# Issuing the decay tables' transfers from ScalarE, ahead of further loads, in a linear-attention and MLP kernel

## Chip, cores and metric

The kernel runs on one core of a Trainium2 chip. The metric is the device time of one execution in microseconds (us). Three runs of the kernel before took 560.29, 560.22 and 559.4 us; the median is 560.22 us.

## What is computed

Three stages stand one behind the other. The first is causal linear attention with decay, for 2 batches of 8 heads, 768 positions and 64 values per head:

```
intra = (q_b k_b^T * Dmask) v_b            # Dmask[i, j] = lam ** (i - j), zero above the diagonal
inter = (q_b * lam ** (i + 1)) kv_state
kv_state = lam ** block * kv_state + (k_b * lam ** (block - 1 - j))^T v_b
```

Each head has its own `lam`, between 0.97 and 0.99. The 1536 x 512 result goes through a gated layer, `(x w_a * x w_b) w_out` with 1536 hidden columns, and through a second layer, `max(x w1, x w2, x w3) w_out` with 768. All is float32; the weights reach the kernel as raw 64-bit words.

## The kernel before, in words

Attention works in 12 chunks (`order`): 2 batches of 6 chunks of 128 positions, all 8 heads at once. A chunk needs four tiles of 256 KB: queries and keys with the head dimension on the partitions (`q`, `k`), keys with positions on the partitions (`n`) and values (`v`). For chunk n, `scores(n)` (L145) multiplies q and k on TensorE; `masked(n)` (L173) multiplies the scores by the decay mask `dmask` on VectorE, one half (even heads, odd heads) at a time, into two tiles `a`; `side(n)` (L156) makes the decayed queries `qs` (from `ltab`) and keys `kd` (from a column of `dmask`) on GpSimd; `values(n)` (L183) multiplies `a` by v (L190), adds the decayed queries times the running state `st` (L194), and makes the state's update `kv` from kd and v (L200). Behind it ScalarE copies the output tile (`xh`, L206), VectorE takes the remainder (`xl`, L207) and sums the state (`std`, L211 or L213), and ScalarE copies it to `st` (L215), which the next chunk's L194 reads. In TensorE's order the first three scores stand first, then values of chunk 0, scores of chunk 3, values of chunk 1, scores of chunk 4, and so on. VectorE's order is the masks of chunks 0, 1 and 2 (six instructions) before `xl` and `std` of chunk 0. Below, q0, k0 and so on are the loads of chunk 0, and "scores of chunk 4" is `scores(4)`.

From chunk 3 on VectorE, ScalarE and GpSimd also split weight tiles into two parts each (L72 to L81), and from chunk 5 on the first layer's products (`up1`, L92) are laid between the chunks. Behind attention only the layers' matmuls are left, with the splits beside them.

The decay tables start from `lam` (L310). `powers()` computes on VectorE a table `tab` of 8 x 256 values (L104 to L113) and stores it to DRAM as `tab_d` (L114, 8 KB). `tables()` (L119) reads it back in shifted windows, as two halves of `dmask`, each 128 partitions with 4 runs of 512 bytes (L122). `decay_rows()` (L124) reads rows broadcast over 64 partitions, twice, into `ltab` (L126).

Every transfer is issued by SyncE (SP in the profile) in the order of the program. The order is written out by hand (`manual_schedule`, from L309). At the head of the program it is: lam, q0, k0, q1, k1, q2, tab_d, k2, v0, the two mask halves, n0, q3, k3, the two `ltab` halves, v1, n1, v2, n2; then, from the loop, q4, k4, v3, n3, and so on.

Two kinds of wait stand ahead of an issue. One is for data: the store of `tab_d` waits for VectorE, and the first mask transfer waits until `tab_d` has landed. The other comes from the framework: it gives the transfers eight completion semaphores in turn, in the order of the program and counted over all issuing engines of this kind together (SyncE and ScalarE), and a transfer that takes up a semaphore waits until the transfer eight before it has landed. An engine that waits at one issue holds back all that it issues behind it.

Of the kernel before, what the change touches and what calls it, by code (L numbers as in the profile page):

```python
# [16 lines left out]
C = 128  # L17
NC = S // C
NP = H // 2
# [14 lines left out]
def decay_attention_gated_mlps(ctx: ExitStack, tc: tile.TileContext, qkv: bass.AP, lam: bass.AP, wts: bass.AP, out: bass.AP):  # L34
    nc = tc.nc
# [13 lines left out]
    def rd(t):  # L49
        return t.bitcast(F32)  # L50

# [1 line left out]
    raw, split = {}, {}  # L53
    state = {"raw": 0, "split": 0}

# [6 lines left out]
            state["raw"] += 1  # L62

    def split_to(u):
        """float64 to float32, bit by bit; what is below float32's normal numbers, told by the upper word read as a float32, becomes zero."""
        while state["split"] <= min(u, NUNIT - 1):
            n = state["split"]
            load_to(n)
            bits = raw.pop(n).bitcast(I32).rearrange("p (n two) -> p n two", two=2)
            low, high = bits[:, :, 0], bits[:, :, 1]  # L70
            w = wp.tile([128, 512], I32, tag="w", name=f"w{n}")
            nc.vector.tensor_scalar(out=w, in0=high, scalar1=3, scalar2=0x3FFFFFF8, op0=ALU.logical_shift_left, op1=ALU.bitwise_and)  # L72
            nc.vector.scalar_tensor_tensor(out=w, in0=low, scalar=29, in1=w, op0=ALU.logical_shift_right, op1=ALU.bitwise_or)  # L73
            nc.vector.scalar_tensor_tensor(out=w, in0=high, scalar=-0x40000000, in1=w, op0=ALU.bitwise_and, op1=ALU.bitwise_or)  # L74
            size = wp.tile([128, 512], F32, tag="s", bufs=2, name=f"ws{n}")
            nc.scalar.activation(out=size, in_=high.bitcast(F32), func=AF.Abs)  # L76
            t = w.bitcast(F32)
            nc.vector.scalar_tensor_tensor(out=t, in0=size, scalar=SMALLEST, in1=t, op0=ALU.is_ge, op1=ALU.mult)  # L78
            hi, lo = t2k(f"wh{n}", F32R), t2k(f"wl{n}", F32R)
            nc.scalar.activation(out=hi, in_=t, func=AF.Copy)  # L80
            nc.gpsimd.tensor_tensor(out=lo, in0=t, in1=rd(hi), op=ALU.subtract)  # L81
            split[n] = (hi, lo)
            state["split"] += 1

    def passes(out_ap, terms):
        """Sum of products of operands in two parts each, without the part below float32."""
        todo = []
        for (wh, _), (xh, xl) in terms:
            todo += [(wh, xh), (wh, xl)]
        todo += [(wl, xh) for (_, wl), (xh, _) in terms]  # L90
        for n, (w, x) in enumerate(todo):
            nc.tensor.matmul(out_ap, w, x, start=n == 0, stop=n == len(todo) - 1)  # L92

# [1 line left out]
    lam_sb = const.tile([H, 1], F32, name="lam_sb")  # L95
    tab = const.tile([H, 2 * C], F32, name="tab")
    pw = const.tile([H, 16], F32, name="pw")
# [2 lines left out]
    tab_d = dp.tile([H, 2 * C], F32, name="tab_d")  # L100

    def powers():
        """tab[h, C - 1 + n] = lam ** n; pw holds lam ** m - 1 for m = 1, 2, 4, ..."""
        nc.vector.memset(tab[:, 0:C - 1], 0.0)  # L104
        nc.vector.memset(tab[:, C - 1:C], 1.0)
        nc.vector.tensor_scalar(out=pw[:, 0:1], in0=lam_sb, scalar1=-1.0, scalar2=None, op0=ALU.add)
        o, m, n = C - 1, 1, 0
        while m < C:
            r = pw[:, n:n + 1]
            nc.vector.scalar_tensor_tensor(out=pw[:, n + 1:n + 2], in0=r, scalar=2.0, in1=r, op0=ALU.add, op1=ALU.mult)  # L110
            nc.vector.scalar_tensor_tensor(out=tab[:, o + m:o + 2 * m], in0=tab[:, o:o + m], scalar=r, in1=tab[:, o:o + m], op0=ALU.mult, op1=ALU.add)
            m, n = 2 * m, n + 1
        nc.vector.tensor_scalar(out=tab[:, o + m:o + m + 1], in0=pw[:, n:n + 1], scalar1=1.0, scalar2=None, op0=ALU.add)  # L113
        nc.sync.dma_start(out=tab_d, in_=tab)  # L114

    def view(offset, ap):
        a = tab_d[:, :]
        return bass.AP(tensor=a.tensor, offset=a.offset + offset, ap=ap)

    def tables():  # L120
        for g in range(2):
            nc.sync.dma_start(out=dmask[:, g], in_=view(g * 2 * C, [[1, 128], [4 * C, NP], [1, C]]))  # L122

    def decay_rows():  # L124
        for hh in range(2):
            nc.sync.dma_start(out=ltab[64 * hh:64 * hh + 64], in_=view(hh * 2 * C + C, [[0, 64], [4 * C, NP], [1, C]]))  # L126

# [1 line left out]
    x = [(xp.tile([128, KD, TT], F32R, tag="x", name=f"xh{t}"), xp.tile([128, KD, TT], F32R, tag="x", name=f"xl{t}")) for t in range(NTT)]  # L129
    st = const.tile([128, NP, 128], F32, name="st")  # L130
    std = const.tile([128, NP, 64], F32, name="std")
# [4 lines left out]
    def load(n, *which):  # L136
        if n >= len(order):
            return
        b, c = order[n]
        for i in which:  # L140
            t = t2k(f"{('q', 'k', 'n', 'v')[i]}{n}")
            nc.sync.dma_start(out=t, in_=qkv[b * NC + c, i])
            ld.setdefault(n, [None] * 4)[i] = t
# [10 lines left out]
        sc[n] = banks  # L154

    def side(n):  # L156
        """What a chunk needs besides its scores: queries and keys times powers of lam."""
        if n >= len(order):
            return
        b, c = order[n]  # L160
        q, k, kn, v = ld[n]
        kd = qs = None
        if c > 0:
            qs = t2k(f"qs{n}")
            nc.gpsimd.tensor_tensor(out=qs, in0=q, in1=ltab.rearrange("p a i -> p (a i)"), op=ALU.mult)
        if c < NC - 1:
            kd = t2k(f"kd{n}")
            nc.gpsimd.tensor_tensor(
                out=kd.rearrange("p (h d) -> p h d", h=H), in0=kn.rearrange("p (h d) -> p h d", h=H),
                in1=dmask[:, :, :, C - 1:C].rearrange("p g a i -> p (g a) i").to_broadcast([128, H, D]), op=ALU.mult)  # L170
        ld[n] = (qs, kd, v)
# [44 lines left out]
            if c < NC - 2:  # L216
                nc.vector.tensor_tensor(out=stt, in0=std, in1=ltab[:, :, C - 1:C].to_broadcast([128, NP, 64]), op=ALU.mult)

# [1 line left out]
    def split_psum(ps, hi, lo):  # L220
        nc.scalar.activation(out=hi, in_=ps, func=AF.Copy)
        nc.vector.tensor_tensor(out=lo, in0=ps, in1=rd(hi), op=ALU.subtract)
# [84 lines left out]
            nc.sync.dma_start(out=out[i * 128:i * 128 + 128, s], in_=ob[:, s])  # L307

    with tc.manual_schedule():  # L309
        nc.sync.dma_start(out=lam_sb, in_=lam)  # L310
        for n in range(2):
            load(n, 0, 1)
        load(2, 0)
        warm = t2k("warm", BF16)
        nc.vector.memset(warm, 0.0)
        nc.scalar.activation(out=warm[:, 0:1], in_=warm[:, 0:1], func=AF.Copy)
        ps = bank("warm_ps")
        for i in range(9):
            nc.tensor.matmul(ps, warm[:, 0:128], warm, start=True, stop=True)
        nc.gpsimd.memset(st, 0.0)  # L320
        powers()
        load(2, 1)
        load(0, 3)
        tables()
        load(0, 2)
        load(3, 0, 1)
        decay_rows()
        load(1, 3, 2)
        load(2, 3, 2)
        for n in range(3):  # L330
            scores(n)
        for n in range(2):
            masked(n)
            side(n)
        plan = [(f, t) for t in range(NTT) for f in range(4)] + [(f, t) for f in range(4, K1) for t in range(NTT)]
        for n in range(len(order)):
            load(n + 4, 0, 1)
            load(n + 3, 3, 2)
            load_to((-1, 0, 1, 2, 4, 6, 8, 9, 10, 11, 12, 13)[n])
            if n > 0:  # L340
                scores(n + 2)
            side(n + 2)
            masked(n + 2)
            values(n)
            for i in range(2):
                split_to((-1, -1, -1, 0, 1, 3, 5, 7, 9, 10, 11, 12)[n] - 1 + i)
                if n >= 5 and i == 0:
                    up1(*plan.pop(0))
        for f, t in plan:
            room = 2 * f + (58 - 3 * (f + 1)) // 2  # L350
            split_to(max(2 * f + 1, min(state["split"], room)))
            load_to(state["split"] + 1)
            if f == K1 - 1 and t > 0:
                split_g(0, 2 * t - 2)
                split_g(0, 2 * t - 1)
            up1(f, t)
            if t == NTT - 1:
                for v in (2 * f, 2 * f + 1):
                    split.pop(v)
        u = 2 * K1  # L360
        for t in range(NTT):
            down1(t, u, 2)
        for k in range(K1):
            split.pop(u + k)
        u += K1
        for f in range(K2):
            split_to(u + 3 * f + 2)
            for t in range(NTT):
                split_to(u + 3 * f + (3 + t if f < K2 - 2 else 3 + 2 * t if f < K2 - 1 else 6 + t))
                load_to(u + 3 * f + 6 + 2 * t)  # L370
                up2(f, t, u)
            for i in range(3):
                split.pop(u + 3 * f + i)
        u += 3 * K2
        for i in range(NT // 128):
            split_to(u + 5)
            down2(i, u)
# [47 lines left out]
```

## Time and profile before

| | us |
|---|---|
| median of three runs | 560.22 |
| lowest and highest run | 559.4, 560.29 |
| profiled execution, span from first to last instruction | 558.3 |
| TensorE busy in it | 541.5 |
| VectorE busy | 289.0 |
| ScalarE busy | 161.0 |
| GpSimd busy | 103.6 |

For the profiled execution only the span is recorded; the times of the runs also hold what lies around the span, 1.92 us at the median. A "busy" TensorE is not one at its peak, since its matmuls are pipelined. The times below are us from the start of the span. A transfer "lands" when its completion is seen; its issue is the short instruction on the queue of the engine that starts it (SPq for SyncE).

### The profile page before, as it was taken

The page shows a single profiled execution, that of the slowest core. Times are in us where ns is not written, and L with a number is a line of the kernel's source. Part 1 is how long each engine was busy: PE and PEld are TensorE (multiplying, and loading weights), DVE is VectorE, ACT ScalarE, POOL GpSimd, SP SyncE. Part 2 cuts the span into 40 slices and gives each one's busy share as a digit, 9 for nine tenths or more (in the row PEclk, how much of TensorE's full clock was granted, in tenths as well). Part 3 has the DMA queues.
Part 4 walks back from the last instruction along what each step waited for, and adds up shares of the span by engine and source line. Part 5 has one row for each costly group of instructions (what it writes and reads, how often), then busy time and mean ns, then how long its engine had stood idle before and what let it go on. Part 6 is the DMA issues. An engine that isn't in the chain of part 4 may idle for free.

```text
span 558.3 us, 7132 instructions
## 1 busy us (share of the span) xinstructions
PE 541.5 (97%) x2811; PEld 446.1 (80%) x2811; DVE 289.0 (52%) x452; ACT 161.0 (29%) x286; POOL 103.6 (19%) x85
## 2 busy tenths in 40 slices
PE   6998889999999999999999999999999999999997
PEld 3876677888888888888888888888888888888886
DVE  2788887676555542134748264124545556774000
ACT  1343334332323322123325152212232323332111
POOL 0735342222212220000110000000011112221000
PEclk9899999999999999999999999999999999999999
DMA  7986442232322321000211111001122112211112
GB/s 226 348 324 217 160 143 76 101 111 92 113 84 105 101 89 38 1 38 1 75 76 38 39 38 39 0 1 38 39 75 77 61 54 98 91 38 38 58 60 73
DMA packets 19089, 48.44 MB, mean 87 GB/s; under 512 B 2024, under 2 KB 3824, under 8 KB 19056
## 3 DMA queue, kind: packets, MB, share of 16 engines
q1 hardware_dynamic: 19056, 47.99, 24.8%
q8 instruction: 22, 0.36, 0.3%
q14 instruction: 11, 0.09, 0.0%
HBM read 44.83 MB, written 3.15 MB: 86 GB/s over the span
## 4 chain that ended last, share of the span: by engine, by line
PE 87%; DVE 5%; DMA 4%; issue 2%; ACT 1%; POOL 1%; SPq 1%; DVEq 0%; POOLq 0%; ACTq 0%
PE p L92 26%; PE y L269 18%; PE pa L92 16%; PE pb L92 16%; PE out L302 9%; DMA k<-qkv_dram 3%; DVE w L72 1%; PE o L194 1%; DVE w L73 1%; DVE w L74 1%; PE o L190 1%; DMA tab_d<-tab 1%; DVE w L78 1%; PE s L153 1%; POOL wl L81 0%
## 5 line engine op out<-in xcount | busy, mean ns | idle before, releaser
L81 POOL TENSOR_TENSOR wl<-w,wh 128x512 fp32r<-128x512 f32 x60 | 78.3, 1305 | 389.4 <-ACT wh L80 288.1
L80 ACT ACTIVATE wh<-w 128x512 fp32r<-128x512 f32 x60 | 37.9, 632 | 192.5 <-DVE w L78 185.5
L92 PE MATMUL p<-yh,wh 128*128 128x512 f32 x216 | 84.0, 389 | 0.0
L92 PE MATMUL p<-yl,wh 128*128 128x512 f32 x216 | 84.0, 389 | 0.0
L244 DVE TENSOR_TENSOR g<-pb,ac 128x512 f32<-128x512 f32 x36 | 24.9, 692 | 85.8 <-PE pb L92 70.7
L92 PE MATMUL pb<-xh,wh 128*128 128x512 f32 x144 | 56.4, 392 | 4.7 <-ACT wh L80 4.7
L92 PE MATMUL p<-yh,wl 128*128 128x512 f32 x216 | 57.7, 389 | 0.0
L92 PE MATMUL pa<-xh,wh 128*128 128x512 f32 x144 | 56.8, 395 | 0.6 <-ACT wh L80 0.5
L92 PE MATMUL pa<-xl,wh 128*128 128x512 f32 x144 | 56.1, 390 | 0.0
L92 PE MATMUL pb<-xl,wh 128*128 128x512 f32 x144 | 56.1, 389 | 0.0
L269 PE MATMUL y<-gh,wh 128*128 128x512 f32 x144 | 56.0, 389 | 0.0
L269 PE MATMUL y<-gl,wh 128*128 128x512 f32 x144 | 56.0, 389 | 0.0
L269 PE MATMUL y<-gh,wl 128*128 128x512 f32 x144 | 56.0, 389 | 0.0
L92 PEld LDWEIGHTS p<-yl,wh 128*128 128x128 f32 x216 | 40.6, 188 | 8.5
L92 PEld LDWEIGHTS p<-yh,wl 128*128 128x128 f32 x216 | 40.5, 188 | 8.4
L92 PEld LDWEIGHTS p<-yh,wh 128*128 128x128 f32 x216 | 40.5, 188 | 8.4
L74 DVE SCALAR_TENSOR_TENSOR w<-wr,w 128x512 int32<-128x512 int32 x60 | 46.1, 769 | 2.0
L78 DVE SCALAR_TENSOR_TENSOR w<-ws,w 128x512 f32<-128x512 f32 x60 | 41.5, 692 | 6.2
L73 DVE SCALAR_TENSOR_TENSOR w<-wr,w 128x512 int32<-128x512 int32 x60 | 42.5, 709 | 2.1
L76 ACT ACTIVATE ws<-wr 128x512 f32<-128x512 f32 x60 | 39.6, 660 | 0.2
L92 PE MATMUL pa<-xh,wl 128*128 128x512 f32 x144 | 38.5, 389 | 0.0
L92 PE MATMUL pb<-xh,wl 128*128 128x512 f32 x144 | 38.5, 389 | 0.0
(61 smaller groups left out, 729.2 us busy)
## 6 DMA issues: line engine op xcount, KB each, us to landing
wr<-wts_dram SPq DMA_DIRECT2D x60, 512.0 KB, 3.3
q<-qkv_dram SPq DMA_DIRECT2D x12, 256.0 KB, 4.6
k<-qkv_dram SPq DMA_DIRECT2D x12, 256.0 KB, 5.1
v<-qkv_dram SPq DMA_DIRECT2D x12, 256.0 KB, 5.9
n<-qkv_dram SPq DMA_DIRECT2D x12, 256.0 KB, 6.0
out_dram<-ob SPq DMA_DIRECT2D x11, 256.0 KB, 2.0
dmask<-tab_d SPq DMA_DIRECT2D x2, 256.0 KB, 4.5
ltab<-tab_d SPq DMA_DIRECT2D x2, 128.0 KB, 6.3
```

Of the source, the lines that this page charges most:

```text
L72: nc.vector.tensor_scalar(out=w, in0=high, scalar1=3, scalar2=0x3FFFFFF8, op0=ALU.logical_shift_left, op1=ALU.bitwise_and)
L73: nc.vector.scalar_tensor_tensor(out=w, in0=low, scalar=29, in1=w, op0=ALU.logical_shift_right, op1=ALU.bitwise_or)
L74: nc.vector.scalar_tensor_tensor(out=w, in0=high, scalar=-0x40000000, in1=w, op0=ALU.bitwise_and, op1=ALU.bitwise_or)
L76: nc.scalar.activation(out=size, in_=high.bitcast(F32), func=AF.Abs)
L78: nc.vector.scalar_tensor_tensor(out=t, in0=size, scalar=SMALLEST, in1=t, op0=ALU.is_ge, op1=ALU.mult)
L80: nc.scalar.activation(out=hi, in_=t, func=AF.Copy)
L81: nc.gpsimd.tensor_tensor(out=lo, in0=t, in1=rd(hi), op=ALU.subtract)
L92: nc.tensor.matmul(out_ap, w, x, start=n == 0, stop=n == len(todo) - 1)
L153: nc.tensor.matmul(banks[h % 2][:, o], k[r:r + 64, o], q[r:r + 64, o], start=True, stop=True)
L244: nc.vector.tensor_tensor(out=gg, in0=pb, in1=a, op=ALU.mult)
L269: nc.tensor.matmul(ps[e], w, m, start=k == 0 and n == 0, stop=k == K1 - 1 and n == 2)
L302: nc.tensor.matmul(ps, a[:, o:o + 128], w[:, s], start=k == 0 and n == 0, stop=k == K2 - 1 and n == 2)
```

## The change

`lam`, the store of `tab_d`, the two mask halves and the two `ltab` halves are issued by ScalarE. The masks' issue moves ahead of the loads of k2 and v0, and these loads change places: v0 and n0 now come before k2. (The diff also takes out comments.)

```diff
 def powers():
     ...
-        nc.sync.dma_start(out=tab_d, in_=tab)
+        nc.scalar.dma_start(out=tab_d, in_=tab)

 def tables():
         for g in range(2):
-            nc.sync.dma_start(out=dmask[:, g], in_=view(g * 2 * C, [[1, 128], [4 * C, NP], [1, C]]))
+            nc.scalar.dma_start(out=dmask[:, g], in_=view(g * 2 * C, [[1, 128], [4 * C, NP], [1, C]]))

 def decay_rows():
         for hh in range(2):
-            nc.sync.dma_start(out=ltab[64 * hh:64 * hh + 64], in_=view(hh * 2 * C + C, [[0, 64], [4 * C, NP], [1, C]]))
+            nc.scalar.dma_start(out=ltab[64 * hh:64 * hh + 64], in_=view(hh * 2 * C + C, [[0, 64], [4 * C, NP], [1, C]]))

     with tc.manual_schedule():
-        nc.sync.dma_start(out=lam_sb, in_=lam)
+        nc.scalar.dma_start(out=lam_sb, in_=lam)
         for n in range(2):
             load(n, 0, 1)
         load(2, 0)
         ...
         powers()
+        tables()
+        load(0, 3, 2)
         load(2, 1)
-        load(0, 3)
-        tables()
-        load(0, 2)
         load(3, 0, 1)
         decay_rows()
         load(1, 3, 2)
         load(2, 3, 2)
```

The order over both engines is then: lam, q0, k0, q1, k1, q2, tab_d, the two masks, v0, n0, k2, q3, k3, the two `ltab` halves, v1, n1, v2, n2, and from there as before. Counted by eights, v0 waits for q0, n0 for k0, k2 for q1, q3 for k1, k3 for q2, the second `ltab` half for the first mask, and v1 for the second mask (before: for v0).

## Rows read from the trace of the kernel before

**Rows 1.** Page, part 1: busy us, share of the span, instructions of each engine.
```profile
PE 541.5 (97%) x2811; PEld 446.1 (80%) x2811; DVE 289.0 (52%) x452; ACT 161.0 (29%) x286; POOL 103.6 (19%) x85
```

**Rows 2.** Windows, four stages: length, each engine's busy us (instructions), PEclk, DMA, GB/s.
```profile
0.00:22.00 22.00, 15.70 (x151) 11.45 (x153) 9.67 (x32) 3.51 (x6) 6.21 (x10) 0.92 0.85 260
22.00:36.00 14.00, 13.48 (x199) 11.56 (x196) 10.87 (x21) 5.61 (x12) 8.25 (x8) 1.00 1.04 392
36.00:80.00 44.00, 37.84 (x303) 30.06 (x304) 38.87 (x53) 15.96 (x30) 19.96 (x16) 1.00 0.52 183
80.00:558.30 478.30, 474.47 (x2166) 393.06 (x2164) 229.63 (x349) 135.97 (x239) 69.17 (x53) 1.00 0.18 61
```

**Rows 3.** Chain of waits, first 22 us: start, length, what.
```profile
0.74 1.32 DMA lam_sb<-lam_dram
...
4.21 3.55 DMA tab_d<-tab
...
9.85 6.25 DMA k<-qkv_dram
...
16.11 5.40 DMA k<-qkv_dram
```

**Rows 4.** Timeline of SyncE's queue: start, length, issue.
```profile
0.74 0.40 SPq L310 DMA_DIRECT2D lam_sb<-lam_dram  x1
1.20 0.36 SPq L142 DMA_DIRECT2D q<-qkv_dram  x1
...
4.21 0.29 SPq L114 DMA_DIRECT2D tab_d<-tab  x1
...
7.85 0.93 SPq L122 DMA_DIRECT2D dmask<-tab_d  x2
...
10.32 1.49 SPq L126 DMA_DIRECT2D ltab<-tab_d  x2
```

**Rows 5.** DMA issues at 7.8 and 8.3 us: size, us from issue to landing.
```profile
dmask<-tab_d SPq DMA_DIRECT2D x1, 256.0 KB, 4.3
dmask<-tab_d SPq DMA_DIRECT2D x1, 256.0 KB, 4.7
```

**Rows 6.** Windows: first loads, masks' transfer, `ltab`'s transfer, TensorE behind its wait.
```profile
2.00:8.40 6.40, 6.11 (x29) 3.33 (x31) 2.06 (x16) 0.22 (x2) 0.00 (x0) 1.00 0.89 286
8.80:12.00 3.20, 1.34 (x24) 1.15 (x22) 0.00 (x0) 0.00 (x0) 0.00 (x0) 1.00 0.72 183
14.60:17.40 2.80, 2.55 (x32) 2.15 (x29) 2.51 (x5) 0.79 (x2) 0.32 (x1) 0.59 1.09 218
15.20:18.20 3.00, 2.79 (x32) 2.44 (x28) 2.33 (x5) 1.19 (x3) 0.62 (x1) 0.50 1.06 276
```

**Rows 7.** Timeline of TensorE: start, us, instruction [idle before <-releaser].
```profile
6.24 3.90 PE L153 MATMUL s<-q,k 64*128 64x128 f32 x48
13.03 0.43 PE L190 MATMUL o<-a,v 128*64 128x128 f32 x2 [2.89 <-DVE a L179]
13.84 1.09 PE L190 MATMUL o<-a,v 128*64 128x128 f32 x14 [0.38 <-DVE a L179]
...
16.23 2.08 PE L153 MATMUL s<-q,k 64*128 64x128 f32 x16 [0.21 <-DMA k<-qkv_dram]
...
19.38 1.16 PE L194 MATMUL o<-qs,st 128*128 128x128 f32 x8
...
21.65 1.16 PE L153 MATMUL s<-q,k 64*128 64x128 f32 x16 [0.49 <-DMA k<-qkv_dram]
...
62.49 0.50 PE L92 MATMUL pb<-xh,wh 128*128 128x512 f32 x1 [1.57 <-ACT wh L80]
```

**Rows 8.** Timelines of ScalarE, VectorE and GpSimd.
```profile
17.20 0.85 ACT L215 ACTIVATE st<-std 64x256 f32<-64x256 f32 x2 [1.64 <-DVE std L211]
...
12.29 3.89 DVE L179 TENSOR_TENSOR a<-s,dmask 128x512 f32<-128x512 f32 x6 [8.10 <-DMA dmask<-tab_d]
...
17.58 1.55 POOL L165 TENSOR_TENSOR qs<-q,ltab 128x512 f32<-128x512 f32 x1 [2.66 <-DMA ltab<-tab_d]
```

## Prediction, made before the change was built or run

> **What bounds the kernel now.** I read the page first: TensorE is busy for 541.5 of 558.3 us [rows 1], so at most 16.8 us are to be had from its waits. The windows then say where those lie [rows 2]: 6.30 us (22.00 - 15.70) before 22 us, 0.52 to 36, 6.16 from there to 80, where VectorE is busy for 38.87 of 44 us, and 3.83 in the 478 us behind. So from 22 us on the program runs by the work of TensorE, then of VectorE, then of TensorE again. Nothing of that work is edited. What the change can give is an earlier start of the run of work that begins near 22 us, and I take such a shift to reach the end whole.
>
> The third view is the timeline of TensorE [rows 7]. The reader should see three waits: 2.89 us before 13.03 and 0.38 before 13.84, both for masked scores `a`, and 0.49 before 21.65, for k4. VectorE's first mask instruction starts at 12.29 [rows 8]; the mask halves, issued at 7.85 and about 8.27 [rows 4], land 4.3 and 4.7 us later, at 12.15 and 12.97 [rows 5]. Ahead of that lies the chain [rows 3]: lam lands at 2.06, the table is stored at 4.21 and has landed at 7.77, and until then SyncE, which issued the table's store at 4.21, then k2 and v0, can issue nothing more: the mask's wait stands in its queue till 7.85 [rows 4]. Behind it, k3 is issued at 9.85 and lands 6.25 later, at 16.10; k4's issue at 16.11 follows that landing at once, since it takes up k3's semaphore, and k4 lands at 21.51 [rows 3].
>
> A fourth view, windows, shows the clock [rows 6]: from 15.2 to 18.2 us the granted clock is 0.50, the lower of the two levels (1.2 and 2.4 GHz), after the wait from 10.14 to 13.03. Scores of chunk 3 took 2.08 us in it; scores of chunk 4 took 1.16 at full clock [rows 7].
>
> **The change part by part.**
>
> *lam on ScalarE.* SyncE's first load starts at 0.74 in place of 1.20, and all five first loads 0.46 earlier [rows 4]. ScalarE's table load now stands behind an issue. No row shows an issue by ScalarE; SyncE's took from 0.29 (tab_d) to 0.75 (half of the 1.49 for two `ltab`) [rows 4]. I take 0.40, that of lam itself. Table load, warm-up matmuls and the first three scores then slide by 0.40 and the scores end near 10.54 in place of 10.14 (6.24 + 3.90 [rows 7]). That costs nothing while masks are what TensorE waits for afterwards. Without that cover it would cost 0.3 to 0.75.
>
> *The table's store.* It leaves the queue in which five loads are ahead of it. Its landing lies between the 1.32 us of lam, with nothing ahead, and the 3.55 us it takes now [rows 3]: 5.5 to 7.8. It still meets loads in the engines, so I take 2.3, near the middle: 6.5, about 1.3 earlier than 7.77.
>
> *The masks.* ScalarE issues them at about 6.55 in place of 7.85. Their first bytes came at 8.8, 0.95 after the issue, so now at 7.5. Meanwhile SyncE, without the table's wait, has issued ten loads: v0, n0, k2, q3 and k3 each wait only for one of the first five. At the 286 GB/s of the first loads [rows 6], from 1.55 on (2.0 less 0.46), 1.70 MB or 6.5 loads of 262 KB are through at 7.5; 3.5 remain beside the masks. Loads need 2.4 us for these at the 392 GB/s of a full stretch [rows 2], 3.2 us at 286. The masks took 3.2 us with the engines 0.72 busy [rows 6], which is 2.3 us of engine time. The second mask can land no earlier than if the loads fit wholly into the masks' gaps (7.5 + 3.2 and the 0.97 from 12.0 to its landing at 12.97: 11.7), and no later than if all runs one behind the other at the slow rates (7.5 + 3.2 + 3.2 + 0.97: 14.9). I take the engine times added, 7.5 + 2.3 + 2.4 = 12.2, and 0.3 for the landing: 12.5, or 0.47 earlier than 12.97, the row that it is nearest to. The first half I put near 11.7.
>
> *What is queued behind the new waits.* On ScalarE: the second `ltab` half waits for the first mask, and behind it stands `xh` of chunk 0, due at about 14.4; it is free. On SyncE: v1 now waits for the second mask (12.5), and behind it stand n1, v2, n2, q4 and k4, whose own conditions are met by then. These six loads need 4.0 us at 392 GB/s after 0.95 to the first bytes; `ltab` adds what it costs now: in the 2.8 us from 14.6, at 218 GB/s, 610 KB moved [rows 6], of which 262 were `ltab`; the other 348 need 0.9 us at 392 GB/s, which leaves 1.9 for `ltab`. Of that 0.95 falls into v1's start-up. So k4 lands near 18.4 (12.5 + 0.95 + 4.0 + 0.95), in place of 21.51, and at 19.4 if nothing does. `ltab` lands near 15.5 at the latest, and GpSimd's `qs` of chunk 1 (1.55 us, now begun at 17.58 [rows 8]) is ready by 17.1.
>
> *TensorE.* The odd heads of chunk 0 start 0.87 behind the second mask's landing (13.84 - 12.97): 13.37. Two things follow side by side. VectorE ends its six masks, `xl` and `std`, and ScalarE ends `st` at 18.05 (17.20 + 0.85 [rows 8]), 5.08 behind that landing: now 17.58. L194 with the `kv` behind it takes 1.78 (19.38 to 21.65, less the wait of 0.49), so `kv` alone 0.62 beside L194's 1.16. TensorE is through the odd heads of chunk 0 (1.09), `kv`, scores of chunk 3 (1.16 at full clock) and L190 of chunk 1 (1.25, sixteen fourteenths of 1.09) at 17.5, all from [rows 7]. So L194 of chunk 1 starts near 17.7, in place of 19.38, and scores of chunk 4 1.78 later, at 19.5, where k4 has been there for 1.1 us, or just arrives. Before, it was 21.65. **Sum:** 2.15 us earlier. Of this 0.47 is the mask, 0.49 k4's wait, and the rest the half clock, which this path does not have. What is late next is the TensorE work itself, then VectorE from 36 us on.
>
> A rule speaks against the change: the Trainium skill, page "DMA: Bandwidth & Descriptors", section "Issuing engines are not separate DMA queues", says that transfers from several engines run on the same 16 engines and interleave, and that issuing from more than one saves only the sequencer's issue time. The trace has only SyncE's queue and can't show it. By it the masks would be no faster for the second queue; that is the second rival.
>
> The span would be 558.3 - 2.15 = 556.15 us. The runs' median stands 1.92 us above the span (560.22 - 558.3), which gives 558.1 us.
>
> **The rivals.**
>
> *The clock falls all the same.* For it: TensorE would still wait from 10.54 to about 12.6 and 0.4 us before 13.37, some 2.5 us against 3.27 now. Against it: a wait of 1.57 us at 62.49 [rows 7] left the granted clock at 1.00, as the stage from 36 to 80 shows [rows 2]. Then scores of chunk 3 start at 15.1, and L194 of chunk 1 follows 3.15 later, as it does now (16.23 to 19.38 [rows 7]), and some 0.5 more, since less of that stretch lies behind the clock's rise: 18.75, and scores of chunk 4 at 20.55. Gain 1.1: 559.1 us.
>
> *The masks come no earlier.* For it: the ten loads that SyncE now issues at once lie in the engines when the masks' 1024 short runs arrive, while now the masks had them nearly alone (183 GB/s in all [rows 6]). Then the second mask lands at 12.97 again, the clock falls as it does now, L194 starts at 19.38, and only k4's wait goes: gain 0.49, 559.7 us. The page's section "Queues, rings and completion order" has each engine take turns between its queues packet by packet, which would give the masks a turn but a small share; no run here shows it.
>
> *Slower: the masks starve.* If they are served behind the loads, at the late end of the bounds, the second lands at 14.9. TensorE then stands idle from 10.54 to 15.77, and comes back at half clock: the odd heads take 1.9 us and `kv` 1.1 (each near twice its length), and with the clock back, scores of chunk 3 and L190 take 1.16 and 1.25, L194 and `kv` 1.78: scores of chunk 4 start at 22.9, 1.2 us later than now: 561.4 us. It decides from a landing of about 13.7 on; v1's new wait for that mask then holds back all further loads too.
>
> *Taken back later.* In the stage from 36 to 80 us VectorE's work and GpSimd's fall on each other differently, and the shift is lost: 560.2 us.
>
> **How the numbers follow.** Forecast 0.42, clock 0.20, masks no earlier 0.22, slower 0.08, taken back 0.08. This kernel's measurement can tell 0.2%, 1.1 us, from no change. The forecast's own range is 557.2 (mask at 11.7, gain 3.0) to 558.8. Faster by more than 0.2% are the forecast and over half of the clock's case: 0.54. Slower by more is most of the starving case: 0.07. The rest, 0.39, is within 0.2%. The range of 8 in 10 leaves out the earliest masks and the starving case: 556.9 to 560.4.
>
> **What would show it.** Right: `tab_d` landing by 7, the second mask by 12.7, scores of chunk 4 starting before 20 without a wait for k4, a granted clock of 1.00 from 15 to 18, and the stages behind as long as before. Wrong: a mask landing past 13, v1's issue leaving the DMA engines empty for over 1 us behind it, `st` or `qs` of chunk 1 later than 18, or VectorE's stage between scores of chunk 4 and 80 us longer by what the start gained.

## The result, and the profile after

The changed kernel is slower: 564.03 us at the median against 559.88 for the kernel before, run beside it; ratio 1.0063, 95% interval 1.0049 to 1.0077. By the ratio the loss is 3.5 us, by the two medians 4.15. The forecast was 558.1 us, the range ended at 560.4, and the case that came, slower by more than 0.2%, was the one given 0.07. The profiled execution took 564.31 us, its span 562.5 (before: 558.3), so 1.81 lie around the span.

The windows of the changed kernel, in the order length, PE, PEld, VectorE, ScalarE, GpSimd, PEclk, DMA share, GB/s, for the stages of [rows 2]:

```profile
0.00:22.00 22.00, 11.34 (x91) 7.69 (x91) 6.46 (x26) 2.09 (x3) 3.88 (x8) 0.84 0.91 275
22.00:36.00 14.00, 13.85 (x202) 11.99 (x203) 11.49 (x20) 5.45 (x12) 8.54 (x8) 1.00 1.01 368
36.00:80.00 44.00, 37.26 (x315) 29.74 (x315) 38.90 (x56) 16.12 (x31) 19.53 (x16) 1.00 0.53 183
80.00:562.50 482.50, 478.67 (x2209) 396.47 (x2207) 233.73 (x353) 137.42 (x242) 71.19 (x55) 1.00 0.18 60
```

TensorE does 4.36 us less before 22 us (15.70 to 11.34), and the last stage is 4.2 us longer; the DMA engines, meanwhile, moved more in the first 22 us than before (275 against 260 GB/s). The loss lies ahead of 22 us, and it isn't a lack of bytes. The timeline of TensorE answers to [rows 7]:

```profile
6.88 3.98 PE L153 MATMUL s<-q,k 64*128 64x128 f32 x48
16.93 0.69 PE L190 MATMUL o<-a,v 128*64 128x128 f32 x2 [6.08 <-DVE a L179]
19.15 1.76 PE L190 MATMUL o<-a,v 128*64 128x128 f32 x13 [1.53 <-DVE a L179]
...
21.91 1.16 PE L153 MATMUL s<-q,k 64*128 64x128 f32 x16
...
25.73 1.16 PE L153 MATMUL s<-q,k 64*128 64x128 f32 x16
```

The wait for the first masked scores is 6.08 us in place of 2.89, that for the odd heads 1.53 in place of 0.38. Scores of chunk 4, without a wait for k4 now, start at 25.73 in place of 21.65: 4.08 us later, and the span is 4.2 longer. Two steps of the chain of waits carry it (start, length, what; before in [rows 3] and [rows 5]):

```profile
4.34 5.29 DMA tab_d<-tab
...
10.12 8.19 DMA dmask<-tab_d
```

The store of the table takes 5.29 us to land in place of 3.55, and the second mask 8.19 in place of 4.7. So the mask lands at 18.31, not 12.97. The queue of SyncE, and that of ScalarE behind it, show what else was under way:

```profile
3.06 0.43 SPq L142 DMA_DIRECT2D v<-qkv_dram  x1
3.53 0.43 SPq L142 DMA_DIRECT2D n<-qkv_dram  x1
4.00 0.43 SPq L142 DMA_DIRECT2D k<-qkv_dram  x1
4.48 0.43 SPq L142 DMA_DIRECT2D q<-qkv_dram  x1
...
6.19 0.34 SPq L142 DMA_DIRECT2D v<-qkv_dram  x1
8.31 0.33 SPq L142 DMA_DIRECT2D n<-qkv_dram  x1
9.67 0.33 SPq L142 DMA_DIRECT2D v<-qkv_dram  x1
10.34 0.33 SPq L142 DMA_DIRECT2D n<-qkv_dram  x1
11.70 0.33 SPq L142 DMA_DIRECT2D q<-qkv_dram  x1
16.11 0.33 SPq L142 DMA_DIRECT2D k<-qkv_dram  x1
...
4.34 0.28 ACTq L114 DMA_DIRECT2D tab_d<-tab  x1
9.65 0.99 ACTq L122 DMA_DIRECT2D dmask<-tab_d  x2
```

Eight loads, to k2 at 4.00, are issued before the store at 4.34, where before there were five. And loads go on beside the masks: n1 goes out just ahead of them, v2, n2 and q4 while they are in flight. The count of semaphores given with the change, ahead of the prediction, is wrong here. The framework does not hand them out in the order of the statements: it merges the two engines' instructions in an order of its own. Worked out from which landing each issue follows (k4 that of the first mask, n3, at 18.33, that of the second), it is one in which v0, n0 and k2 come before `tab_d`, and v1, n1 and v2 before, between and behind the masks. So v1 does not wait for the second mask; the first load that waits for a mask is k4, which SyncE holds until 16.11. The DMA queues from 9.6 to 18.4 us (packets, MB, share of 16 engines; q1 is SyncE's, q10 ScalarE's):

```profile
q1 hardware_dynamic: 951, 1.72, 68.7%
q10 hardware_dynamic: 1593, 0.78, 36.9%
```

In the 8.7 us in which masks and `ltab` (0.78 MB) were to be moved, 1.72 MB of loads went through the same engines.

### The profile page after: what moved, and what is told of

Same layout as the page of the kernel before. It is cut to its first block, busy times and chain, and to the rows that moved or that the text cites. A ratio compares the mean times of both kernels' runs of the same rounds, so it can differ in the third digit from the quotient of the medians.

```text
span 562.5 us, 7133 instructions
## 1 busy us (share of the span) xinstructions
PE 541.1 (96%) x2811; PEld 445.9 (79%) x2811; DVE 290.6 (52%) x452; ACT 161.1 (29%) x286; POOL 103.1 (18%) x85
## 4 chain that ended last, share of the span: by engine, by line
PE 85%; DVE 7%; DMA 3%; issue 3%; ACT 1%; POOL 1%; ACTq 0%; DVEq 0%; POOLq 0%
PE p L92 26%; PE y L269 17%; PE pa L92 15%; PE pb L92 15%; PE out L302 9%; DMA dmask<-tab_d 1%; DVE w L72 1%; DVE w L73 1%; DVE w L74 1%; PE o L190 1%; DVE a L179 1%; PE o L194 1%; DMA tab_d<-tab 1%; DVE w L78 1%; PE s L153 1%
```

## The experiments

Ten kernels were run, each beside the kernel before. Theory A has two halves: A1, loads issued before the table's store delay its landing, on whichever queue it is; A2, loads issued beside or behind the masks slow the masks. Its rivals: B, the new order of the loads; C, ScalarE's queue itself; and that lam's move costs.

**The queue alone.** The changed kernel with the statements in their old order:

```diff
         powers()
-        tables()
-        load(0, 3, 2)
         load(2, 1)
+        load(0, 3)
+        tables()
+        load(0, 2)
```

> The five transfers on ScalarE as in the changed kernel, but the statements in their old order (k2, v0, masks, n0, q3, k3). Theory A, backlog: SyncE, no longer stopped by the table, puts as many loads ahead of tab_d as in the changed kernel (eight by 4.3 us), so tab_d takes about 5.3 us to land again, the second mask lands near 18 us, and the time is 563 to 564.5 us. Theory B, the new order of loads is at fault (v0 and n0 ahead of k2): the time is back within 1 us of 559.9.

Measured: 563.99 us, ratio 1.0076 (1.0051 to 1.0101). `tab_d` landed at 9.46 and the second mask at 17.70:

```profile
4.90 4.56 DMA tab_d<-tab
9.95 7.75 DMA dmask<-tab_d
```

So the loss comes with the move to ScalarE's queue, not with the order; the store itself went out 0.56 later here (lam took 2.00 us to land), and took 4.56, under the 5.3 expected, with nine loads ahead.

**The order alone.** The changed kernel with all six issues back on SyncE, such as:

```diff
-        nc.scalar.dma_start(out=tab_d, in_=tab)
+        nc.sync.dma_start(out=tab_d, in_=tab)
```

> The new order of statements alone, all transfers on SyncE. Theory A, backlog: only five loads stand ahead of tab_d, it lands in 3.4 to 3.7 us, the masks go next and alone and land in under 5 us each, by 12.5; k2 then comes behind the masks and v0, n0, near 14.5, and scores of chunk 2 hold the values of chunk 0 back by 1 to 2 us, so 560 to 562 us. Theory B, order at fault: 563 to 564.5.

Measured: 561.80 us, ratio 1.0035 (1.0023 to 1.0046). The store lands in 3.36 us, the first mask in 4.2, the second near 13.1 (VectorE goes on at 13.14), as late as in the kernel before. What costs is k2, which comes behind the masks and holds scores of chunk 2, and with them the values of chunk 0:

```profile
15.14 2.08 PE L153 MATMUL s<-q,k 64*128 64x128 f32 x16 [6.07 <-DMA k<-qkv_dram]
```

The order has a price of its own here, 2 us. In the changed kernel it is not what is waited for: there k2 goes out at 4.00, as nothing holds it.

**SyncE held until the table has landed.** The changed kernel with a small transfer on SyncE that reads `tab_d`:

```diff
         tables()
+        nc.sync.dma_start(out=gate_sb, in_=tab_d[:, 0:2])
         load(0, 3, 2)
```

> The changed kernel with one small transfer more on SyncE (8 x 2 values read from tab_d) ahead of v0, so that SyncE stops behind its first five loads until tab_d has landed, as it did before; tab_d, masks and ltab stay on ScalarE. Theory A, backlog: tab_d lands in 3.4 to 3.7 us, near 7.9; the masks are issued at once, with only v0, n0 and k2 beside them, and the second lands by 14; 559 to 561 us. Theory C, ScalarE's queue is itself the slow one (its transfers get a small turn, whatever is ahead): tab_d still takes 5 us or a mask over 6, and 562.5 to 564.5 us.

Measured: 562.51 us, ratio 1.0053 (1.0036 to 1.0070), above the range of A and within that of C, but not for C's reason. The store, 4.92 to 6.69, and the masks, the second landing near 12.8, are earlier than in the kernel before; k2 is what comes late:

```profile
4.92 1.77 DMA tab_d<-tab
8.04 7.42 DMA k<-qkv_dram
```

I had left out of this expectation the cost of k2 behind the table, which I had put into the one before.

**The backlog on one queue.** All on SyncE, but eight loads ahead of the store and q3, k3, v1 ahead of the masks:

```diff
+        load(0, 3, 2)
+        load(2, 1)
         powers()
-        tables()
-        load(0, 3, 2)
-        load(2, 1)
         load(3, 0, 1)
+        load(1, 3)
+        tables()
         decay_rows()
-        load(1, 3, 2)
+        load(1, 2)
```

> All on SyncE, but with the changed kernel's backlog: eight loads (to k2) ahead of tab_d, q3, k3 and v1 ahead of the masks, ltab behind the masks, n1 and the rest behind that. Theory A, backlog: tab_d takes 5 to 5.5 us on this queue too, as in the changed kernel, since it lands when the loads issued before it have; the masks then have nothing issued after them in their way and land in 4.5 to 5.5 us, the second by 15.2; 561 to 562.5 us. Theory C, the second queue is what slows: tab_d lands in under 4.5 us here.

Measured: 561.43 us, ratio 1.0038 (1.0025 to 1.0051).

```profile
4.99 4.53 DMA tab_d<-tab
9.96 5.03 DMA dmask<-tab_d
```

With SyncE's queue alone and eight loads ahead the store lands at 9.52, between the times from ScalarE's queue with eight or nine (9.63 and 9.46 above, 10.09 in a run below). Its 4.53 us are under the 5 to 5.5 expected by A and just over C's 4.5, but it also went out 0.65 later than in the changed kernel. The queue gives it no lead that shows beside this spread. Nor does it land behind the whole of the load issued just ahead of it: k2 arrives half a us later, as TensorE's wait shows:

```profile
10.09 1.16 PE L153 MATMUL s<-q,k 64*128 64x128 f32 x16 [1.28 <-DMA k<-qkv_dram]
```

The masks, with only `ltab` close behind them and n1 and the rest behind that, all in one queue, land in 5.03, and of the 4.2 us by which the changed kernel's span is longer 1.9 are left (560.2 against 558.3).

**The masks alone on ScalarE's queue.** The changed kernel, with SyncE held behind v1 until both masks are there:

```diff
         load(3, 0, 1)
+        load(1, 3)
+        nc.sync.dma_start(out=gate_d[:, 0:1], in_=dmask[0:1, 0, 0, 0:1])
+        nc.sync.dma_start(out=gate_d[:, 1:2], in_=dmask[0:1, 1, 0, 0:1])
         decay_rows()
-        load(1, 3, 2)
+        load(1, 2)
```

> The changed kernel, with SyncE held behind v1 until both mask halves have landed (two transfers of 4 bytes that read the masks); everything ahead of the masks, their backlog and their queue (ScalarE's) stay as in the changed kernel. Theory A2, the loads issued after the masks share the engines with them: alone the masks land in 4.3 to 5.3 us in place of 6.4 and 8.2, the second by 15.3, scores of chunk 4 start by 23.6 in place of 25.7, and the time is 561 to 562.3 us. Theory C, ScalarE's queue is itself slow: the second mask still takes over 6.5 us and the time stays at 563 us or more.

Measured: 561.46 us, ratio 1.0026 (1.0014 to 1.0037). Chain of waits, the two queues from 9.6 to 15 us, and TensorE's start of scores of chunk 4 (L153 is L158 in this kernel):

```profile
4.33 5.76 DMA tab_d<-tab
10.55 4.32 DMA dmask<-tab_d
...
q10 hardware_dynamic: 1593, 0.78, 56.8%
q1 hardware_dynamic: 287, 0.50, 24.4%
...
23.11 1.16 PE L158 MATMUL s<-q,k 64*128 64x128 f32 x16
```

The queue, the backlog and the store's late landing are those of the changed kernel, a little worse; n1, v2, n2 and q4 are gone from beside the masks (0.50 MB of loads moved in these 5.4 us, 1.26 in the changed kernel's), and the second mask takes 4.32 in place of 8.19. This settles C: ScalarE's queue is not slow. It is also the size of A2: scores of chunk 4 start 2.62 us earlier than in the changed kernel (25.73).

**lam and the store alone.** The kernel before with two lines changed, all else as it was:

```diff
-        nc.sync.dma_start(out=tab_d, in_=tab)
+        nc.scalar.dma_start(out=tab_d, in_=tab)
         ...
-        nc.sync.dma_start(out=lam_sb, in_=lam)
+        nc.scalar.dma_start(out=lam_sb, in_=lam)
```

> The kernel before with lam and the store of tab_d alone on ScalarE; masks, ltab and all order as before, so SyncE still stops at the masks and nothing can overtake them. Theory A1, the loads issued ahead of the store delay it: k2 and v0 now go out before it, seven loads in place of five, and tab_d takes 4.0 to 4.4 us in place of 3.4 to 3.6; the masks take 4.2 to 4.9 as before, the second lands near 13.7, and the time is 560.4 to 561.2 us. Rival D, only the sharing during the masks matters: 559.4 to 560.1, no change.

Measured: 560.78 us, ratio 1.0025 (1.0009 to 1.0041).

```profile
4.22 4.19 DMA tab_d<-tab
...
22.26 1.16 PE L153 MATMUL s<-q,k 64*128 64x128 f32 x16 [0.60 <-DMA k<-qkv_dram]
```

Here the masks are as in the kernel before (4.3 and 4.7 us), nothing overtakes them, and still it is slower: k2 and v0 now go ahead of the store, which takes 4.19 in place of 3.55. That is A1 by itself, 0.6 us at scores of chunk 4.

**Old order, held at the table.** The changed kernel with k2 and v0 first, and the small transfer that reads `tab_d` behind them:

```diff
         tables()
-        load(0, 3, 2)
         load(2, 1)
+        load(0, 3)
+        nc.sync.dma_start(out=gate_sb, in_=tab_d[:, 0:2])
+        load(0, 2)
```

> The changed kernel in the old order of loads (k2 and v0 first), with SyncE held behind these seven loads until tab_d has landed; masks on ScalarE, with n0, q3 and k3 free to go beside them. A1 and A2 together: tab_d takes 4.0 to 4.4 us with seven loads ahead, the second mask 5.3 to 6.5 with three loads beside it, landing near 14.5; 561 to 562 us. Theory B, the order of the loads is what matters: 559.4 to 560.3 us.

Measured: 560.54 us, ratio 1.0019 (1.0009 to 1.0029), between the ranges of the two theories: the store took 3.85, the second mask 5.0 with n0, q3 and k3 beside it, both less than expected. Three loads beside the masks on the other queue make little difference: 5.0 here and 5.6 in the run held at the table, against 4.7 to 5.2 in the kernels with the same or like loads right behind the masks on one queue. The 8.19 of the changed kernel came with 1.72 MB, more than six loads.

**lam back on SyncE.** The changed kernel with one line as before:

```diff
-        nc.scalar.dma_start(out=lam_sb, in_=lam)
+        nc.sync.dma_start(out=lam_sb, in_=lam)
```

> The changed kernel with lam back on SyncE. The warm-up matmuls start at 2.3 in place of 2.9 us, and the first loads 0.46 later. All theories here: the time stays at 563 to 564.5 us, since the masks are waited for long after; if lam's move were what costs, it would fall below 562.

Measured: 563.22 us, ratio 1.0063 (1.0048 to 1.0078): lam's place is not what costs. The table landed earlier (8.44), since with lam first on SyncE the loads go out later and k2 falls behind the store, so that seven loads are ahead of it:

```profile
4.21 0.55 ACTq L114 DMA_DIRECT2D tab_d<-tab  x1
4.43 0.43 SPq L142 DMA_DIRECT2D k<-qkv_dram  x1
```

The second mask still took 7.12 us, and scores of chunk 4 began at 24.43.

**Two tries at a faster kernel.** By A1, fewer loads ahead of the store should help. First q2 moved behind it, all on SyncE; then v0 behind the masks as well (the second cut is against the first kernel):

```diff
         for n in range(2):
             load(n, 0, 1)
-        load(2, 0)
         ...
         powers()
-        load(2, 1)
+        load(2, 0, 1)
         load(0, 3)
         tables()
```

> The kernel before, all on SyncE, with q2 moved behind the store of tab_d: four loads ahead of it in place of five. Theory A1: tab_d lands in 2.7 to 3.1 us, near 7.0; the masks are issued 0.7 us earlier, but q2, k2 and v0 stand in the queue ahead of them, so the second lands only 0.2 to 0.5 earlier, near 12.6; 559.0 to 559.6 us beside 559.5, within what can be told. If the loads ahead don't matter, tab_d still takes 3.4 us or more.

```diff
         load(2, 0, 1)
-        load(0, 3)
         tables()
-        load(0, 2)
+        load(0, 3, 2)
         load(3, 0, 1)
```

> As the run with q2 behind the store, and v0 behind the masks too: q2 and k2 alone stand between tab_d and the masks. Theory A1 and A2: tab_d lands near 7.0, the second mask near 11.9 with nothing beside it, v0 in one queue behind it near 12.5, and scores of chunk 4 start 0.6 to 1.2 us earlier than 21.65; 558.3 to 559.0 us, faster than both kernels. If the mask is not what sets it, 559.5 or more (v0 late, or k4).

Measured: 559.65 us for the first, ratio 0.9996 (0.9986 to 1.0005), no change that can be told; its store took 3.08. The second gave 560.75, ratio 1.0011 (1.0001 to 1.0021), where 558.3 to 559.0 was expected, though its store landed in 2.38 us and its second mask at 12.4, earlier than before. What it gained there went to the next transfers in the queue; `ltab` landed at 17.71, `stt` and `qs` waited for it, and scores of chunk 3 took 2.08 us again, at half clock:

```profile
10.49 7.22 DMA ltab<-tab_d
...
17.84 0.43 DVE L217 TENSOR_TENSOR stt<-std,ltab 128x256 f32<-128x256 f32 x1 [1.19 <-DMA ltab<-tab_d]
```

No kernel tried beats the one before.

**All together.** "Start" is that of scores of chunk 4, and the last column is the span less it.

| kernel | loads ahead of the store | store, us to landing | second mask, us to landing | start | span | span less start |
|---|---|---|---|---|---|---|
| before | 5 | 3.55 | 4.7 | 21.65 | 558.3 | 536.7 |
| changed | 8 | 5.29 | 8.19 | 25.73 | 562.5 | 536.8 |
| queue alone | 9 | 4.56 | 7.75 | 25.36 | 562.2 | 536.8 |
| backlog on SyncE | 8 | 4.53 | 5.03 | 23.49 | 560.2 | 536.7 |
| masks alone | 8 | 5.76 | 4.32 | 23.11 | 560.0 | 536.9 |
| lam and store | 7 | 4.19 | 4.7 | 22.26 | 559.0 | 536.7 |
| old order, held | 7 | 3.85 | 5.0 | 22.36 | 559.0 | 536.6 |
| lam back | 7 | 4.23 | 7.12 | 24.43 | 561.5 | 537.1 |
| order alone | 5 | 3.36 | 5.1 | 23.18 | 560.0 | 536.8 |
| new order, held | 5 | 1.77 | 5.6 | 24.00 | 560.8 | 536.8 |
| q2 behind | 4 | 3.08 | 5.0 | 21.29 | 558.0 | 536.7 |
| q2, v0 behind | 4 | 2.38 | 5.2 | 22.32 | 559.1 | 536.8 |

The starts of "order alone" and "new order, held" are set by k2, not by a mask. The store goes out between 4.21 and 4.99, so its landing compares better than its time: 6.73 and 7.33 with four loads ahead, 6.69 to 7.77 with five, 8.19 to 8.44 with seven, 9.46 to 10.09 with eight or nine. The count ahead is not all: with five ahead and none behind, the store landed at 6.69 and 7.57, with k2 and v0 behind it at 7.77; why, no run shows.

## Why the prediction was wrong, point by point

**What bounds the kernel: right.** The work behind 22 us kept its length. The span less the start of scores of chunk 4 stays between 536.6 and 537.1 us in all twelve kernels, so a shift of either sign reaches the end whole, and "taken back later" fell.

**The table's store: the first step that failed.** I took 2.3 us and gave 3.55 as the upper end, because the store "leaves the queue in which five loads are ahead of it". It took 5.29. The bound was of another situation: with SyncE free of the store's wait, three loads more were out before it. In the next paragraph I counted these loads against the masks, but not against the store. That the queue gives no lead is shown by the backlog run (9.52 on SyncE's queue, 9.46 to 10.09 on ScalarE's). The Trainium skill, "DMA: Bandwidth & Descriptors", section "Queues, rings and completion order", says that a completion is a strongly ordered write, which lands only after all earlier writes of that DMA engine, over all its queues. In the changed kernel the store does land with the load issued just ahead of it (9.63; k2, whose landing let v2 go, by 9.67), but in the backlog run half a us before k2, and with the queue alone 0.8 us before q3 (issued at 4.47, 5.8 us to landing). These are times of whole transfers, not of single engines: they neither bear that rule out nor contradict it, and whether the table's data had landed sooner, no run shows. What the runs show is the landing by the count of loads ahead.

**The masks: the step that failed by most.** Of the 5.34 us by which the second mask is late, 1.86 are the store's (issue and landing), and 3.49 the mask's own flight. I had bounded the landing at 14.9 by counting only the loads issued before the masks, on the ground that v1 would wait for the second mask. That count was wrong, as the queue shows, and v1, n1, v2, n2 and q4 came in addition; the late end was too early by 3.4 us. The run with the masks alone gives the term by itself: 4.32 in place of 8.19 us, 2.62 us of the 4.08 at scores of chunk 4. The rest is A1, as the backlog run and that of lam and store show on their own.

**Which rival it was.** "Slower: the masks starve" had the place and the mechanism right, and the landing too early: it gave 14.9 and 1.2 us. Its path holds: the run with the masks alone has nearly that landing (14.87) and starts scores of chunk 4 at 23.11, where the rival said 22.9. With 18.31 the same sum gives 4.7 us; 4.08 were measured. Its turning point, a landing of about 13.7, is not borne out: with landings of 13.6 (lam and store) and 13.7 (old order, held) scores of chunk 4 were already 0.6 and 0.7 us late, the first with a wait for k4, the second for VectorE. The rival's chance was set too low, since I took as likeliest a value near the middle of the bounds, when the one row of short runs in company (`ltab` beside k3, 218 GB/s [rows 6]) pointed up. The rule quoted in the prediction, that a second queue saves issue time alone (the Trainium skill, "DMA: Bandwidth & Descriptors", section "Issuing engines are not separate DMA queues"), agrees with the runs, which go further: the time saved was cover. While SyncE stood at the masks' wait it kept loads from the engines that the table and the masks needed.

**The clock.** I forecast no half clock. It was 0.50 over a longer stretch than before, behind a longer wait (row of windows):

```profile
15.20:20.80 5.60, 2.34 (x19) 1.94 (x21) 3.08 (x5) 0.00 (x0) 1.95 (x2) 0.50 1.02 258
```

A wait of just 2.5 us in all, as in the forecast, no run had, but the nearest speak against its full clock. With q2 behind the store TensorE waited 2.51 and 0.51 us, and the clock still fell:

```profile
12.77 0.43 PE L190 MATMUL o<-a,v 128*64 128x128 f32 x2 [2.51 <-DVE a L179]
13.71 1.75 PE L190 MATMUL o<-a,v 128*64 128x128 f32 x13 [0.51 <-DVE a L179]
14.00:16.00 2.00, 2.00 (x27) 2.00 (x26) 2.00 (x4) 0.28 (x1) 0.89 (x1) 0.50 1.12 222
```

With the old order, held, it fell behind waits of 2.29 and 1.16, and so it did, in the first 22 us, in each kernel that was run. Of the 2.15 us that I forecast, 1.19 hung on this.

**Smaller steps.** lam on ScalarE cost 0.63 us at the warm-up (issue 0.60, bound 0.75), hidden as said, and the run with lam back shows it. k4 landed 4.1 us after its issue at 16.11, 5.5 us before its scores, so its wait is gone, as forecast, and it was worth nothing.

## What to carry to other kernels

A wait that stops a queue may be what keeps the DMA engines free for the transfer on the critical path; before taking it away, count every load that will then be issued before that transfer and beside it. A second queue was no faster lane here. Where the semaphores of transfers are given out by a framework over several engines, read the waits from the program as built, or from its trace, not from the order of statements.

## What was not expected of the hardware

A store of 8 KB on a queue of its own landed no sooner than on the loaded one: at 9.52 us from SyncE's with eight loads ahead, at 9.46 to 10.09 from ScalarE's with eight or nine. That spread is as large as any difference between the queues. Transfers of 512-byte runs suffer from 2 KB loads beside them: 4.32 us with few of them, 8.19 beside more than six; three made little difference (5.0 and 5.6). And lam's 32 bytes, issued in the same moment as the first loads but from the other queue, took 1.33 to 2.03 us to land; on SyncE, ahead of these loads, 1.32 to 1.46.
